# A planned attention, Fourier and feed-forward kernel on one core: shared work is left to ScalarE or GpSimd where they end it in time, and two batches are transposed earlier

## The chip, the cores and the metric

The kernel runs on one core of a Trainium2 chip. The core has a matrix engine (PE, with weight loads on PEld), a vector engine (DVE), a scalar engine (ACT), GpSimd (POOL) and a queue engine (SP); they run beside each other and wait for each other by semaphores. The metric is the time of one execution in microseconds (us) on the device, less is better; three runs of the kernel before are given by their median.

## The reference

Four batches of 576 tokens, 8 heads of 64, width 512. Attention with random features comes first: `phi(x) = exp(proj - max)`, `kv = k_p^T v`, output `(q_p kv) / (q_p z)`. Two layers follow:

```python
X = np.fft.fft(np.fft.fft(x, axis=1), axis=2)          # layer one
u = x + np.real(X)
un = (u - mean) / sqrt(var + 1e-6)
x = u + relu(un @ w_ch1) @ w_ch2                        # 512 -> 2048 -> 512

h = x.transpose(0, 2, 1) @ U @ V                        # layer two, U 576x32, V 32x576
u = x + h.transpose(0, 2, 1)
out = u + relu(u @ w_ch1) @ w_ch2
```

Weights come as 64-bit floats and are converted on the chip. Every matmul is done in pairs of a high and a low part (`xh`, `xl`), so one product costs three matmuls: high by high, high by low, low by high.

## The kernel before, in words

**Stages.** Attention runs over 36 tiles of 128 tokens (`proj`, `exps`, then `kvmm` for keys, `qtr`, `num` and `xtr` for queries). For query tile n, `pt` transposes phi, a copy to `qpT` on ACT or DVE follows, `pn` multiplies it with kv, DVE divides (`den`, `x`), and `px` transposes the result, which a copy puts into `uT`, the residual (512 x 2304, transposed). The Fourier stage runs as filling work in between: `fold` (z tiles), `ps` and `pdp`/`pdq` matmuls, and DVE or POOL adds into `uT`. The feed-forward part works on six blocks of 384 tokens: 0, 1, 3 and 4 are the first 384 tokens of the four batches, blocks 2 and 5 the last 192 of batches 0 and 1 and of batches 2 and 3. Its first hidden columns run unit by unit (`phu`, `acc`, functions `l1`, `l2`), and all others in cells (`loop`): a cell (J, p) is weight group J on the pair p of blocks, (0, 1), (2, 5) or (3, 4); it has four hidden products of 12 matmuls (`ph`) and seven output products of 6 (`p`), which DVE adds into `uT`. Cells 0 to 17 are layer one, 18 to 35 layer two.

**Between the layers** stands `rec_mix(b)` for each batch b (the two thin products with U and V): for five token tiles PE transposes `uT` (`mt`), ACT writes a high part, DVE the low part, PE adds them up with U (`pg`); then ACT and DVE make `g2`, and eight matmuls with V (`pu`) follow, each added into `uT` by DVE. `pu` has two PSUM banks, so the third waits until DVE has added the first. Then `rec_x2` makes the input tiles `yh` (ACT) and `yl` (DVE or POOL) of a block.

**What sets the order.** No engine schedules itself. Every step is recorded with `add`: a set of engines that may do it with a cost each, and keys that it reads and writes. `Sched.plan` gives each step a latest start (`lst`), counted back from the PE work in its recorded place, then walks through time and lets the engine that is free first take, among the steps that are ready, the one with the smallest `lst`. A step with several engines (a copy on A or V, a subtraction on V or G) goes to whichever takes it. Steps with `lock` on VectorE and GpSimd are kept apart in time. What comes out is a fixed program for each engine. So a changed rule or key moves thousands of instructions.

Of the kernel before, what the change touches and what calls it, by code (L numbers as in the profile page):

```python
# [91 lines left out]
ENGS = "XPAVGSD"  # L92

# [5 lines left out]
class Sched:  # L99
# [8 lines left out]
    def add(self, eng, fn, r=(), w=(), lock=False, main=False, early=0.0, slack=0.0):  # L108
# [5 lines left out]
        o.preds, o.succs, o.raw, o.slack = set(), [], set(), slack  # L114
# [14 lines left out]
        self.ops.append(o)  # L129

    def plan(self):
        ops = self.ops
        for i, o in enumerate(ops):
            for p in o.preds:
                ops[p].succs.append(i)
            o.left, o.on, o.lst, o.after = len(o.preds), None, None, None
# [6 lines left out]
        for o in reversed(ops):  # L143
# [4 lines left out]
            o.lst = (min(v) if v else t) - o.early  # L148
        chain = [i for i, o in enumerate(ops) if o.main]
# [34 lines left out]
        while len(order) < n:  # L184
# [84 lines left out]
def tile_favor_fnet_moe(ctx: ExitStack, tc: tile.TileContext, qT, kT, v1, om, w1a, w2a, uu, vv, w1b, w2b, cs, cd, out):  # L269
# [90 lines left out]
    plb = ca.enter_context(tc.tile_pool(name="plb", bufs=1))  # L360
# [10 lines left out]
    CE = (("ce",), CA)  # L371
    C1 = CE[0]
# [38 lines left out]
    def load(n):  # L411
# [4 lines left out]
        def fn(e):  # L416
# [4 lines left out]
            if n:  # L421
                nc.sync.dma_start(r, src)
# [7 lines left out]
        add({"S": S256 if n else 1.7}, fn, [C1], [("rw", n % 3)] + ([] if n else [("sa",)]))  # L430

    def load_v(n):
# [16 lines left out]
        add({"S": S256}, fn, [C1], [("vt", i % 3)])  # L449

    def om_prep():
        def sc(e):
            nc.scalar.activation(M["omr"], M["omr"], AF.Copy, scale=SCALE)
# [5 lines left out]
        add({"A": 0.32}, sc, [], [("sa",)])  # L459
# [17 lines left out]
    def proj(n, g):  # L477
# [24 lines left out]
        add({"V": V512}, red, [("pj", b), CP, CA], [("mx", n % 2, g)])  # L502

    def exps(n, g):
        if n >= NS:
            return
        for h0 in (4 * g, 4 * g + 2):
# [11 lines left out]
    def kvmm(n, i):  # L519
# [24 lines left out]
    def qtr(n, g):
# [14 lines left out]
        add({"A": 0.49, "V": V512}, cpy, [("pm", q), CE[n % 2], CA], [("qpT", n % 2, g)])  # L559

    def num(n, g):
# [33 lines left out]
        add({"V": 0.08}, div, [bank, CA] + bx, [("den", g)])  # L595
# [29 lines left out]
    def fold(n, src, rk, key):  # L625
# [49 lines left out]
    def s_stage(b, kd, kind):  # L675
# [1107 lines left out]
```

## Time and profile before

| | before |
|---|---|
| median of 3 runs | 1034.96 us (1033.78 to 1038.09) |
| the profiled execution, its span | 1032.16 us, 1030.4 us |
| PE, PEld busy | 98 %, 95 % |
| DVE, ACT, POOL busy | 86 %, 51 %, 37 % |
| matmuls | 6240 |

The span runs from the first to the last instruction; 1.76 us of the execution lie around it. The busy time of PE counts a matmul until its modelled end, so matmuls that follow each other closely overlap (a 128x384 one is shown with 0.34 us but starts 0.17 us after the one before), and an idle stretch of PE is a little shorter in the table than what the wait costs.

### The profile page before, as it was taken

The numbers are of one execution on the slowest core, as the hardware profiler recorded it, in microseconds if no ns is written. First come the engines' busy times: TensorE is split into PE (matmuls) and PEld (weight loads), VectorE is DVE, ScalarE is ACT, GpSimd is POOL, SyncE is SP. The second block draws the span as 40 slices with busy tenths as digits, with TensorE's granted clock in tenths as the row PEclk, the third lists the DMA queues.
The fourth block names the chain that finished last, engine by engine and source line by source line (L and its number), as shares of the span: only waits on it lengthen the run. The fifth ranks groups of instructions, "written<-read, shape, count | busy, mean of one in ns | idle before, by whom it ended". The sixth has DMA issues, their size and how long they took to land.

```text
span 1030.4 us, 17155 instructions
## 1 busy us (share of the span) xinstructions
PE 1007.1 (98%) x6240; PEld 983.6 (95%) x6240; DVE 883.7 (86%) x1906; ACT 522.6 (51%) x1212; POOL 380.2 (37%) x396
## 2 busy tenths in 40 slices
PE   9999999898999999999999999999999999999998
PEld 8999998898999999999999998889999999999997
DVE  5788999677888999989899888998999898987766
ACT  6797888634444443444442565544554354443232
POOL 2266235412414334424332371524543343433211
PEclk9999999999999999999999998999999999999999
DMA  6445230010112110011110201002121111010013
GB/s 190 139 165 164 74 93 11 9 34 21 42 41 86 58 48 10 30 49 35 62 41 21 62 21 42 21 22 83 42 62 41 42 41 63 26 37 1 1 62 122
DMA packets 49091, 57.01 MB, mean 55 GB/s; under 512 B 3120, under 2 KB 42160, under 8 KB 48880
## 3 DMA queue, kind: packets, MB, share of 16 engines
q1 hardware_dynamic: 48720, 53.23, 16.9%
q0 software_dynamic: 288, 2.70, 0.7%
q8 instruction: 49, 0.80, 0.3%
q14 instruction: 34, 0.28, 0.1%
HBM read 51.20 MB, written 4.72 MB: 54 GB/s over the span
## 4 chain that ended last, share of the span: by engine, by line
PE 88%; DVE 7%; ACT 2%; POOL 1%; issue 1%; DMA 0%; SPq 0%; DVEq 0%; ACTq 0%; POOLq 0%
PE ph L1007 11%; PE ph L1008 11%; PE ph L1006 11%; PE p L1267 10%; PE p L1265 10%; PE p L1266 10%; PE pj L397 4%; PE kvp L397 3%; DVE uT L382 2%; PE acc L1043 1%; PE acc L1042 1%; PE acc L1044 1%; PE phu L1006 1%; PE phu L1007 1%; PE phu L1008 1%; PE pn L397 1%
## 5 line engine op out<-in xcount | busy, mean ns | idle before, releaser
L382 DVE TENSOR_TENSOR uT<-uT,p 128x384 f32<-128x384 f32 x588 | 308.3, 550 | 57.0 <-PE p L1267 56.0
L312 POOL TENSOR_TENSOR w<-w,sc 128x512 uint32<-128x512 uint32 x64 | 87.7, 1372 | 149.0 <-DVE w L308 118.3
L1006 PE MATMUL ph<-yh,ah 128*128 128x384 f32 x384 | 130.3, 339 | 0.6 <-ACT yh L388 0.6
L1007 PE MATMUL ph<-yl,ah 128*128 128x384 f32 x384 | 129.9, 338 | 0.7 <-DVE yl L382 0.7
L1008 PE MATMUL ph<-yh,al 128*128 128x384 f32 x384 | 129.9, 338 | 0.0
L1267 PE MATMUL p<-hl,bh_s 128*128 128x384 f32 x294 | 99.6, 339 | 0.2 <-DVE hl L382 0.2
L1265 PE MATMUL p<-hh,bh_s 128*128 128x384 f32 x294 | 99.0, 337 | 0.0
L1266 PE MATMUL p<-hh,bl_s 128*128 128x384 f32 x294 | 98.8, 336 | 0.0
L1006 PE MATMUL ph<-xh,ah 128*128 128x384 f32 x288 | 97.1, 337 | 0.0
L1008 PE MATMUL ph<-xh,al 128*128 128x384 f32 x288 | 96.8, 336 | 0.0
L1007 PE MATMUL ph<-xl,ah 128*128 128x384 f32 x288 | 96.8, 336 | 0.0
L512 ACT ACTIVATE phi<-pj,mx 128x128 f32<-128x128 f32 x288 | 82.5, 386 | 16.6 <-DVE mx L499 16.4
L388 ACT ACTIVATE r<-ph 128x384 f32<-128x384 f32 x66 | 32.5, 492 | 103.1 <-PE ph L1008 103.0
L388 ACT ACTIVATE hh<-t 128x384 fp32r<-128x384 f32 x72 | 37.9, 526 | 82.1 <-DVE t L991 78.9
L382 POOL TENSOR_TENSOR hl<-r,hh 128x384 fp32r<-128x384 f32 x36 | 39.9, 1107 | 100.6 <-ACT hh L388 92.3
L1006 PEld LDWEIGHTS ph<-yh,ah 128*128 128x128 f32 x384 | 72.7, 189 | 1.7 <-ACT yh L388 0.8
L1007 PEld LDWEIGHTS ph<-yl,ah 128*128 128x128 f32 x384 | 72.6, 189 | 1.1 <-DVE yl L382 1.0
L1008 PEld LDWEIGHTS ph<-yh,al 128*128 128x128 f32 x384 | 72.6, 189 | 0.0
L388 ACT ACTIVATE hh<-f 128x384 fp32r<-128x384 f32 x60 | 31.6, 526 | 79.5 <-PE p L1266 25.1
L1265 PE MATMUL p<-hh,bh_a 128*128 128x384 f32 x210 | 71.0, 338 | 0.1
L1266 PE MATMUL p<-hh,bl_a 128*128 128x384 f32 x210 | 70.7, 336 | 0.0
L1267 PE MATMUL p<-hl,bh_a 128*128 128x384 f32 x210 | 70.6, 336 | 0.0
(724 smaller groups left out, 2873.1 us busy)
## 6 DMA issues: line engine op xcount, KB each, us to landing
raw<-in_w1a_dram SPq DMA_DIRECT2D x16, 512.0 KB, 3.7
raw<-in_w2a_dram SPq DMA_DIRECT2D x16, 512.0 KB, 3.7
raw<-in_w2b_dram SPq DMA_DIRECT2D x16, 512.0 KB, 3.5
raw<-in_w1b_dram SPq DMA_DIRECT2D x16, 512.0 KB, 3.7
raw<-in_qT_dram SPq DMA_DIRECT2D x18, 256.0 KB, 3.0
out_dram<-uT SPq DMA_DIRECT2D x24, 192.0 KB, 2.0
raw<-in_kT_dram SPq DMA_DIRECT2D x17, 256.0 KB, 3.0
vt<-in_v_dram SPq DMA_DIRECT2D x16, 260.0 KB, 2.7
```

The lines of the kernel that those rows point to most:

```text
L312: sch.ins = aeng.tensor_tensor(out=mu, in0=mu, in1=s, op=ALU.add).ins
L382: sch.ins = ENG[e].tensor_tensor(out=o, in0=x, in1=y, op=op).ins
L388: nc.scalar.activation(o, x, fn)
L397: nc.tensor.matmul(o, w, m, start=start, stop=stop, skip_group_check=True)
L512: nc.scalar.activation(phi_[n][:, h, :], pj_[(n, g)][:, h - 4 * g, :], AF.Exp, bias=mx_[n][:, h : h + 1])
L1006: nc.tensor.matmul(ph, wh[:, c], xh[:, r, :], start=(r == 0), stop=False)
L1007: nc.tensor.matmul(ph, wh[:, c], xl[:, r, :], start=False, stop=False)
L1008: nc.tensor.matmul(ph, wl[:, c], xh[:, r, :], start=False, stop=(r == 3))
L1042: nc.tensor.matmul(a, wh[:, c], hh, start=(f == 0), stop=False)
L1265: nc.tensor.matmul(a, wh[:, cc], hh, start=first, stop=False, skip_group_check=True)
L1266: nc.tensor.matmul(a, wl[:, cc], hh, start=False, stop=False, skip_group_check=True)
L1267: nc.tensor.matmul(a, wh[:, cc], hl, start=False, stop=True, skip_group_check=True)
```

## The change

**The rule.** In `plan`, VectorE has chosen a step that another engine may also do. If some other engine x would end that step before its latest start (plus what PE is late; ScalarE gets 1.0 us more), VectorE takes the most urgent ready step that only VectorE can do instead. If there is none it keeps the step. `MIX` holds one entry that does nothing.

**The start.** The small matrix `om` is loaded on ScalarE's queue; the loads of input tile 2 and of the first values are recorded behind its scaling.

**Attention.** `xtr` (`px`) is recorded ahead of the second half of `num` (`pn`). Some keys are made finer or added.

**Block 2.** Its layer-one input tiles get an own pool (`xpc`), opened in the place of attention tiles when these are done, where they had to wait for the end of the whole Fourier stage (`close_a`); so `lnu_c(2)` and `lnu_v(2)` are recorded earlier. The tiles `mm` and `pmm` move to another pool.

**Between the layers.** The last two weight groups of layer one are interleaved, so blocks 0 and 1 are done with four cells to go (three before). Batches 0 and 1 get own tiles for the transposes (in the layer-one input tiles of blocks 0 and 1), and their first three token tiles are recorded from there; on PE the three transposes of batch 1 now stand in cell 16 instead of 17, some 115 to 145 matmul instructions earlier. Batches 2 and 3 begin with their last two token tiles.

```diff
+GS = 0.0
+GA = 0.0
+AS = 1.0
...
+            if e == "V" and l > GA and any(max(free[x], avail(i, x)) + o.eng[x] < l + late + (GS if x == "G" else AS) for x in o.eng if x != e):
+                alt = [x for x in now if len(ops[x[1]].eng) == 1]
+                if alt:
+                    l, i, v = min(alt)
+                    o = ops[i]
...
-                if p == 0:
-                    M["omr"] = lnp.tile([128, 512], F32, tag="sa", name="omr")[:, 0:256]
-                    nc.sync.dma_start(M["omr"], om)
...
+    def load_om():
+        def fn(e):
+            M["omr"] = lnp.tile([128, 512], F32, tag="sa", name="omr")[:, 0:256]
+            nc.scalar.dma_start(M["omr"], om)
...
-    cells += [(J, p) for pp in ((0, 1), (2,)) for J in (NP - 2, NP - 1) for p in pp]
+    cells += [(J, p) for p in range(3) for J in (NP - 2, NP - 1)]
...
-        pool = xps[0 if blk < 2 else 1]
+        pool = M["x2"] if blk == 2 else xps[0 if blk < 2 else 1]
...
+    def close_c(e):
+        c2.close()
+        M["x2"] = ctx.enter_context(tc.tile_pool(name="xpc", bufs=1, side="right", reuse_waits="tile"))
...
     def rec_mix(b):
+        own = b < 2
+        order = TILES if own else TILES[3:] + TILES[:3]
...
+            add({"P": 0.3}, tr, [("u", r, b, "h" if t < 3 else "t") for r in range(4)] + [mk], [("m", 1)])
+            add({"A": A512}, nh, [("m", 1), mk], [("nh", k)])
+            add({"V": 0.62}, nl, [("m", 1), ("nh", k), mk], [("nl", k)])
...
+            if own and s == 2:
+                yield
...
+            if (J, p) == (NP - 1, 0):
+                mx = [rec_mix(b) for b in range(4)]
+                for b in (0, 1):
+                    next(mx[b])
             if (J, p) == (NP - 2, 2):
                 for b in (0, 1):
-                    rec_mix(b)
+                    next(mx[b], None)
...
+                if s > 10:
+                    xtr(n - 2)
                 if s > 9:
                     num(n - 1, 1)
                 qtr(n, 1)
                 exps(m, 1)
-                if s > 10:
-                    xtr(n - 2)
...
                 lnu_rs(1)
                 lnu_mean(2)
+                lnu_c(2, True, True)
+                lnu_v(2)
...
-        lnu_c(2, True, True)
-        lnu_v(2)
```

PE has the same 5870 matmul instructions before and after. DVE has 1908 instructions before and 1828 after, ACT 1214 and 1219, POOL 401 and 477. Three places show what moved; in the order the names are those of the program, with the numbers of tile, batch or cell.

PE in the attention stage, query tiles 33 to 35, before (`pt34_0` transposes, `pn33_1` is the second half of the product of tile 33, `pj35_1` the projection of tile 35):

```order
L397 MATMUL pn33_0_2695<-kv3_2118,qpT33_2655 128x65 x4
L609 MATMUL px31_2707<-ident_58,x31_2557 128x128 x3
L609 MATMUL px31_2707<-ident_58,xr31_2609 128x128
L550 MATMUL pt34_0_2718<-ident_58,phi34_2644 128x128 x4
L397 MATMUL pn33_1_2725<-kv3_2118,qpT33_2655 128x65 x4
L397 MATMUL pj35_1_2736<-omh_119,th35_2554 128x256
L397 MATMUL pj35_1_2736<-oml_120,th35_2554 128x256
```

and after:

```order
L570 MATMUL pt34_0_2714<-ident_58,phi34_2644 128x128 x4
L413 MATMUL pj35_1_2727<-omh_115,th35_2525 128x256
L413 MATMUL pj35_1_2727<-oml_116,th35_2525 128x256
L413 MATMUL pj35_1_2727<-omh_115,tl35_2526 128x256
L413 MATMUL pj35_1_2727<-omh_115,th35_2525 128x256
L413 MATMUL pj35_1_2727<-oml_116,th35_2525 128x256
L413 MATMUL pj35_1_2727<-omh_115,tl35_2526 128x256
L629 MATMUL px32_2743<-ident_58,x32_2641 128x128 x3
L629 MATMUL px32_2743<-ident_58,xr32_2725 128x128
L413 MATMUL pn33_1_2750<-kv3_2123,qpT33_2658 128x65 x4
```

The second half `pn33_1` came straight behind `pt34_0`; now the six matmuls of `pj35_1` and the transposes `px32` stand between them.

DVE where the low parts of block 2's input (`xl2`) are made, before (`hht7_0` belongs to unit 7, the last before block 2's first unit 8):

```order
L382 TENSOR_TENSOR hht7_0_3634<-acc4_0_3291,rs1_3196 128x384
L382 TENSOR_TENSOR xl2_3632<-c2_0True_3403,xh2_3631 128x384
L382 TENSOR_TENSOR xl2_3632<-c2_1True_3409,xh2_3631 128x384
L382 TENSOR_TENSOR c2_2True_3643<-uT_67,mean2_3206 128x384
L382 TENSOR_TENSOR c2_3True_3648<-uT_67,mean2_3206 128x384
L382 TENSOR_TENSOR s2_3_3652<-uT_67 128x384
L382 TENSOR_TENSOR q2_0_3411<-q2_0_3411,q2_2_3650 128x384
L382 TENSOR_TENSOR xl2_3632<-c2_2True_3643,xh2_3631 128x384
L382 TENSOR_TENSOR q2_0_3411<-q2_0_3411,q2_3_3656 128x384
L382 TENSOR_TENSOR xl2_3632<-c2_3True_3648,xh2_3631 128x384
```

and after (`hlu3`, `hlu4` are the low hidden parts of units 3 and 4):

```order
L1018 SCALAR_TENSOR_TENSOR hlu3_3192<-phu3_3145,hhu3_3177 128x384
L398 TENSOR_TENSOR xl2_3190<-c2_0True_3179,xh2_3189 128x384
L398 TENSOR_TENSOR c2_2True_3207<-uT_67,mean2_3166 128x384
L398 TENSOR_TENSOR xl2_3190<-c2_1True_3184,xh2_3189 128x384
L398 TENSOR_TENSOR q2_0_3194<-q2_0_3194,q2_1_3205 128x384
L398 TENSOR_TENSOR c2_3True_3222<-uT_67,mean2_3166 128x384
L398 TENSOR_TENSOR q2_0_3194<-q2_0_3194,q2_2_3214 128x384
L398 TENSOR_TENSOR abl_2_3_3132<-ps2_3o_3168,abh_2_3_3131 128x2x144
L398 TENSOR_TENSOR q2_0_3194<-q2_0_3194,q2_3_3236 128x384
L398 TENSOR_TENSOR xl2_3190<-c2_2True_3207,xh2_3189 128x384
L398 TENSOR_TENSOR xl2_3190<-c2_3True_3222,xh2_3189 128x384
```

`xl2` stood behind unit 7; now all four are done before the hidden part of unit 4.

DVE at the end of layer one, from the last adds of cell 17 (`p17`) to the adds of batch 1's `pu1`, before (`w36` and `w39` are weights under conversion):

```order
L382 TENSOR_TENSOR uT_67<-uT_67,p17_0_1_7713 128x384
L915 TENSOR_SCALAR w36_7448<-w36_7448 128x512
L382 TENSOR_TENSOR uT_67<-uT_67,pu1_0_7878 128x288
L382 TENSOR_TENSOR uT_67<-uT_67,pu1_1_7880 128x288
L308 SCALAR_TENSOR_TENSOR w36_7448<-raw36_7394,w36_7448 128x512
L382 TENSOR_TENSOR uT_67<-uT_67,pu1_2_7889 128x288
L382 TENSOR_TENSOR uT_67<-uT_67,pu1_3_7892 128x288
L382 TENSOR_TENSOR uT_67<-uT_67,pu1_4_7899 128x288
L382 TENSOR_TENSOR uT_67<-uT_67,pu1_5_7902 128x288
L911 TENSOR_SCALAR w39_7718<-w39_7718 128x512
L382 TENSOR_TENSOR uT_67<-uT_67,pu1_6_7905 128x288
L382 TENSOR_TENSOR uT_67<-uT_67,pu1_7_7911 128x288
```

and after:

```order
L398 TENSOR_TENSOR uT_67<-uT_67,p17_5_1_7886 128x384
L398 TENSOR_TENSOR uT_67<-uT_67,p17_0_0_7743 128x384
L398 TENSOR_TENSOR uT_67<-uT_67,pu1_1_7917 128x288
L398 TENSOR_TENSOR uT_67<-uT_67,pu1_0_7920 128x288
L398 TENSOR_TENSOR uT_67<-uT_67,p17_0_1_7755 128x384
L398 TENSOR_TENSOR uT_67<-uT_67,pu1_3_7943 128x288
L398 TENSOR_TENSOR uT_67<-uT_67,pu1_2_7945 128x288
L398 TENSOR_TENSOR uT_67<-uT_67,pu1_5_7954 128x288
L398 TENSOR_TENSOR uT_67<-uT_67,pu1_4_7958 128x288
L398 TENSOR_TENSOR uT_67<-uT_67,pu1_7_7963 128x288
L398 TENSOR_TENSOR uT_67<-uT_67,pu1_6_7966 128x288
```

The three conversion steps between the `pu1` adds are gone, and one add of `p17` stands between the first pair and the rest. On PE all eight `pu1` matmuls followed each other behind the 12 of `ph18_0`; now two stand behind the first three of these 12, and six behind all of them.

## Rows read from the trace of the kernel before

**Rows 1.** The page: an engine's busy time, and the chain that ended last.

```profile
PE 1007.1 (98%) x6240; PEld 983.6 (95%) x6240; DVE 883.7 (86%) x1906; ACT 522.6 (51%) x1212; POOL 380.2 (37%) x396
...
PE 88%; DVE 7%; ACT 2%; POOL 1%; issue 1%; DMA 0%; SPq 0%; DVEq 0%; ACTq 0%; POOLq 0%
```

**Rows 2.** Windows: start:end, length, busy of PE, PEld, DVE, ACT, POOL (instructions), clock, DMA.

```profile
0.00:100.00 100.00, 95.32 (x787) 92.25 (x788) 72.20 (x167) 76.40 (x232) 43.51 (x56) 1.00 0.54 166
150.00:200.00 50.00, 44.46 (x357) 41.09 (x357) 39.18 (x107) 39.45 (x108) 22.14 (x24) 1.00 0.04 11
200.00:250.00 50.00, 48.32 (x306) 47.04 (x305) 37.21 (x86) 19.31 (x42) 12.04 (x19) 1.00 0.11 33
250.00:300.00 50.00, 47.63 (x276) 45.35 (x275) 45.14 (x96) 23.09 (x50) 14.07 (x13) 1.00 0.14 43
300.00:600.00 300.00, 300.00 (x1725) 297.26 (x1724) 272.45 (x577) 131.57 (x272) 115.13 (x111) 1.00 0.14 43
600.00:650.00 50.00, 47.84 (x256) 42.50 (x255) 44.65 (x92) 31.61 (x65) 18.70 (x19) 0.93 0.14 43
650.00:700.00 50.00, 47.44 (x267) 43.85 (x266) 46.06 (x98) 23.55 (x49) 20.14 (x20) 1.00 0.05 13
700.00:1000.00 300.00, 300.00 (x1719) 299.79 (x1719) 258.27 (x533) 131.19 (x268) 111.70 (x109) 1.00 0.13 42
```

**Rows 3.** Timeline of the start: start, length, engine, line, operation, count, idle before and releaser.

```profile
7.63 0.42 DVE L382 TENSOR_TENSOR oml<-omr,omh 128x256 fp32r<-128x256 f32 x1
...
7.96 0.68 DVE L499 TENSOR_REDUCE mx<-pj 128x4 f32<-128x512 f32 x1
...
9.88 0.38 PE L397 MATMUL pj<-omh,th 128*128 128x256 f32 x1 [0.92 <-ACT phi L512]
```

**Rows 4.** Waits of PE, 60 to 240 us: total, times, longest.

```profile
PE px L609 <- DVE abl L382: 1.8, 2, 1.4
PE pt L550 <- ACT phi L512: 1.4, 3, 0.8
```

**Rows 5.** Timeline of PE at block 2's first hidden product.

```profile
252.04 0.45 PE L1006 MATMUL phu<-xh,ah 128*128 128x384 f32 x1
...
257.66 0.34 PE L1006 MATMUL phu<-xh,ah 128*128 128x384 f32 x1
```

**Rows 6.** Timeline of PE at two `pu` stretches and behind the second.

```profile
603.14 0.43 PE L1496 MATMUL pu<-vh,mxl 96*128 96x288 f32 x2
603.41 0.34 PE L1006 MATMUL ph<-xh,ah 128*128 128x384 f32 x1
```

**Rows 7.** Timeline of PE at batch 1's `pu` and the first `yh` of block 1.

```profile
625.81 0.43 PE L1496 MATMUL pu<-vh,mxl 96*128 96x288 f32 x2
...
630.76 1.11 PE L1454 MATMUL mt<-ident,uT 128*128 128x128 f32 x4 [0.55 <-DVE uT L382]
631.52 0.67 PE L1006 MATMUL ph<-yh,ah 128*128 128x384 f32 x1
...
635.51 0.68 PE L1454 MATMUL mt<-ident,uT 128*128 128x128 f32 x4
```

**Rows 8.** Timeline of DVE beside it.

```profile
627.14 0.69 DVE L308 SCALAR_TENSOR_TENSOR w<-raw,w 128x512 uint32<-128x512 uint32 x1
627.74 1.80 DVE L382 TENSOR_TENSOR uT<-uT,pu 128x288 f32<-128x288 f32 x4
629.47 0.42 DVE L911 TENSOR_SCALAR w<-w 128x512 f32<-128x512 f32 x1
```

**Rows 9.** Window behind it, columns as in rows 2.

```profile
631.50:635.50 4.00, 4.00 (x14) 3.91 (x13) 3.73 (x8) 2.16 (x4) 0.00 (x0) 0.50 0.00 0
```

**Rows 10.** Groups by line and form: count, busy us, mean ns, idle before.

```profile
L382 DVE TENSOR_TENSOR uT<-uT,p 128x384 f32<-128x384 f32 x588 | 308.3, 550 | 57.0 <-PE p L1267 56.0
...
L382 DVE TENSOR_TENSOR hl<-r,hh 128x384 fp32r<-128x384 f32 x60 | 35.6, 593 | 5.6 <-ACT hh L388 5.5
```

**Rows 11.** The same view, of POOL.

```profile
L382 POOL TENSOR_TENSOR hl<-r,hh 128x384 fp32r<-128x384 f32 x36 | 39.9, 1107 | 100.6 <-ACT hh L388 92.3 <-issue 6.5 <-DVE hl L382 1.1
```

More of the change, by code (lines that the diff above doesn't have):

```diff
@@ L106, in __init__, with add @@
         self.ins = None
-    def add(self, eng, fn, r=(), w=(), lock=False, main=False, early=0.0, slack=0.0):
+    def add(self, eng, fn, r=(), w=(), lock=False, main=False, early=0.0, slack=0.0, after=None):
         if not self.on:
@@ L133, in plan @@
         for i, o in enumerate(ops):
+            if o.after is not None:
+                o.preds.add(o.after)
             for p in o.preds:
                 ops[p].succs.append(i)
[L136 removed]
+            o.left, o.on, o.lst = len(o.preds), None, None
         t = 0.0
@@ L148, in plan @@
             o.lst = (min(v) if v else t) - o.early
+        for i, o in enumerate(ops):
+            k = max(j for j in range(len(MIX)) if MIX[j][0] <= o.lst)
+            if MIX[k][1] and not o.main:
+                o.lst += MIX[k][2] * (((i + 1) * 2654435761 + MIX[k][1] * 2246822519) % 65521 / 65521 - 0.5)
         chain = [i for i, o in enumerate(ops) if o.main]
@@ L409, in warm, with load @@
             add({"P": 0.45 * WARM}, fn, [CA], [("pm", 0)])
-    def load(n):
+    def load(n, after=None):
         if n >= NS:
@@ L691, in fn @@
             for c in range(2):
-                zh, zl = zs_[f"{b}{kind}{c}"]
+                zh, zl = (zs_[f"{b}{kind}{c}"][i] for i in range(2))
                 ch = cs_[:, 0, c, i0 : i0 + 2 * w]
@@ L711, in s_stage @@
         add({"P": 1.08}, fn, zk + [("cst",), CA], [("pm", q)])
-        add({"A": 0.3}, hi, [("pm", q), CA], [("abh", sl, kind)])
+        add({"A": 0.3}, hi, [("pm", q), CA], [("abh", sl, kind)] + ([(x, sl, y) for x in ("abh", "abl") for y in "eo"] if kind == "e" else []))
         add({"V": 0.38}, lo, [("pm", q), ("abh", sl, kind), CA], [("abl", sl, kind)])
@@ L1437, in rec_mixc, with tiles, bufs, g2t @@
             add({"V": 0.4}, lambda e, vs=vs: tt("V", b["vh"][64:96, vs], b["vr"][64:96], b["vh"][64:96, vs].bitcast(F32), ALU.subtract), [("sq", 1)], [("vh",)], lock=True)
+    MX = {}
     def rec_mix(b):
         x = {}
[L1442 to L1452 removed]
+        own = b < 2
+        mk = ("mx", b) if own else ("mx", 2)
+        order = TILES if own else TILES[3:] + TILES[:3]
+        def tiles():
+            k = b if own else 2
+            if k not in MX:
+                blk = b if own else 5
+                MX[k] = [xps[0 if own else 1].tile([128, 3, 512], F32R, tag=f"x{i}{blk}", name=f"mx{i}{k}") for i in "hl"]
+            return MX[k]
+        def bufs(s):
+            ta, tb = tiles()
+            if own:
+                return ta[:, s % 3], tb[:, s % 3]
+            return ((ta[:, 0], ta[:, 1]), (ta[:, 2], tb[:, 0]))[s % 2]
+        def g2t():
+            ta, tb = tiles()
+            return ta[0:96, 2] if own else tb[0:96, 1 + b % 2]
+        if b != 3:
+            add({"X": 0.0}, lambda e: tiles(), [], [mk] + [("x", b if own else 5, r) for r in range(4)])
+        nb = 3 if own else 2
+        for s, (t0, n) in enumerate(order):
+            t = t0 // 128
+            if own and s == 3:
+                for q in range(3):
+                    x[q]()
+                x["q"] = 3
+            def tr(e, s=s, t0=t0, n=n):
+                x["pt"] = bank(f"mt{b}_{s}", ("m", 1)).rearrange("p (r d) -> p r d", r=4)
@@ L1477, in gs1 @@
+            x[s] = lambda s=s, k=k, pgm=pgm: add({"P": 0.46}, pgm, [("nh", k), ("nl", k), ("ust",), mk], [("m", 0)])
+            if not (own and s < 3):
+                for q in range(x.get("q", 0), s + 1):
+                    x[q]()
+                x["q"] = s + 1
+            if own and s == 2:
+                yield
         def gs1(e):
@@ L1658, in whole @@
         num(NS - 1, 0)
+        xtr(NS - 2)
         num(NS - 1, 1)
-        xtr(NS - 2)
         for p in fill.get(NS - 1, []):
             p()
+        add({"X": 0.0}, close_c, [], [C2] + [("x", 2, r) for r in range(4)])
         lnu_rs(0)
```

125 lines of the change are left out of this document (60 added, 65 removed).

## The prediction

> **What bounds the kernel now.** I read the page first. PE is busy 98 % of the span, and the chain that ended last runs through PE for 88 % [rows 1]. PE's instructions are the same after the change, so time can be won only where PE waits or runs slowly. The windows show where that is [rows 2]. From 300 to 600 and from 700 to 1000 us PE is busy all the time: nothing to win there, only to lose. It idles 4.7 us in the first 100 us, 5.5 from 150 to 200, 1.7 from 200 to 250, 2.4 from 250 to 300, and 2.2 and 2.6 in the two windows from 600 to 700, where the layers meet. A wait costs more than its idle time, because the overlap of pipelined matmuls is lost: a 128x384 matmul is shown with 0.34 us [rows 5] but follows the one before after 300/1725 = 0.174 us [rows 2], so I add 0.17 us for each wait that goes.
>
> In the stretches with idle time I looked at PE's waits and at the timelines of PE and DVE. The reader is to see there that PE is always held by something short: a copy, a maximum, a subtraction on DVE or ACT that stands too late in its engine's order. DVE is busy 272 of 300 us and 258 of 300 us in the quiet stretches and POOL 115 and 112 [rows 2], so DVE is the engine that is short of room and POOL has some.
>
> **The change part by part.** All terms are sums against the profiled execution of 1032.16 us, which is 2.8 us below the median of 1034.96; I add the 2.8 at the end.
>
> The start. PE waits 0.92 us at 9.88 for an exponential, which waits for the first maximum on DVE at 7.96, and this stands directly behind `oml` at 7.63 (0.33 us from start to start) [rows 3]. In the new order `oml` is DVE's first step, while DVE still waits for input, so the maximum moves up by that 0.33 us; the `om` load no longer stands among SP's first loads, so tile 1's comes up by one issue as well. Against it: ACT issues a DMA before its table load, ACT now also makes tile 2's high part between its first exponentials, and the loads of tile 2 and of the first values wait for ACT's scaling. Bounds: 0.9 lost to 1.3 won. I take 0.8 won.
>
> Attention, 60 to 240 us. PE waits there in many short pieces, the largest two groups being 1.8 us in two waits of `px` and 1.4 us in three waits of `pt` [rows 4]. The order puts the projection (six matmuls) and `px` between `pt` and the second `pn`, so the copy between them has that much longer, and DVE's work becomes more even: in the order, 27 instructions stood between the maxima of tiles 16 and 17 and 28 between those of 34 and 35; now it is 13 and 14. But the waits for the z tiles (`ps` on `zl`) keep about the same distance, and shifting shared steps leaves some of them to POOL, where a subtraction takes 1.11 us on average against 0.59 on DVE [rows 10, 11]. The idle time to be had is 2.2 us before 100 (4.7 less 1.5 for the first instruction and the 0.9 above), 5.5 and 1.7 later, together 9.4 us. Bounds: everything goes (9.4 won, and 0.17 for each of some 17 waits, 12 in all), or new waits of the same size arise elsewhere (0, or 3 lost by a third more). In between no row decides; I take a bit less than half of the 12: 5.3 won.
>
> Block 2. From 252.04 to 257.66 us PE does 12 matmuls and takes 5.62 us [rows 5]; at 0.174 each they take 2.1. The rest, 3.5 us, is waiting for `xl2` and `xh2`, whose tiles came free only with the Fourier stage. In the new order all four `xl2` steps stand before the hidden part of unit 4, while block 2 starts with unit 8: four units of 24 matmuls, some 17 us, lie between. What is late next is `prs2`, needed only when block 2's results are scaled. I take 3.5 won; bounds 2.5 to 3.5.
>
> Between the layers. The eight `pu` of batch 1 and the four transposes behind them take from 625.81 to 631.52, 5.71 us [rows 7]. Their own work is 8 times 0.135 (two took 0.27 in an undisturbed place [rows 6]) and 0.38 for the transposes (half of 0.76, at half clock), together 1.46; 4.25 us are lost, because each pair waits for DVE's two adds, and between these stand steps of weight conversion, which nobody needs soon: 0.60 us for one, from 627.14 to 627.74 [rows 8]. In the new order these are gone, two of the eight are done under cover of `yh0` matmuls, and six remain in a row. Four adds took 1.73 us (627.74 to 629.47) [rows 8], so three pairs take 2.6, with the transposes 3.0 us; their own work is 1.2, so 1.8 us are lost and 2.4 won. While PE stood in these gaps its clock fell: from 631.5 to 635.5 it was granted 0.50, the lower of its two levels, 1.2 GHz [rows 9]. 12 matmuls took 3.99 us there (631.52 to 635.51 [rows 7]) instead of 2.1: 1.9 us. With three pairs in place of four and nine full matmuls behind the first pair I expect PE to stay at 2.4 GHz, so these 1.9 are won too. Should the clock fall all the same, nothing of the 1.9 is won.
>
> For batches 2 and 3 (640 to 681 us) the order keeps `pu` in rows (eight in a row became rows of up to six for batch 3, where it had been three); DVE has as many adds as before. Batch 1's transposes moved out of cell 17 into cell 16, so DVE comes out of cell 17 with 45 instructions where it had 54. I take 0.6 won here. Bounds for the border of the layers as a whole: 1 lost (longer rows at batch 3, the clock falls anyway) to 8 won (all of the 4.7 us idle [rows 2] with nine waits, and the 1.9 of the clock). I take 2.4 + 1.9 + 0.6 = 4.9.
>
> The cells. Some 62 of POOL's 76 additional instructions stand in the cells, mostly low parts of weights, which are made a group ahead, and about 13 `hl` and `yl`, which PE needs soon. The rule hands a step over only if POOL ends it before its latest start on DVE. In the trace PE never waited in the cells although POOL made 36 `hl<-r` there at 1.11 us [rows 2, 11]. I take 0.5 lost for two or three late ones; bounds 0 to the rival below.
>
> Beside POOL, DVE's own `hl<-r` takes 593 ns in the mean where its add of a PSUM result takes 550 [rows 10]; 76 more POOL steps that slow one DVE step each by this 43 ns cost DVE 3 us in all, off PE's path. Against this change stands a rule: the Trainium skill (SBUF — State Buffer, Who interferes with whom) says that a VectorE instruction with two SBUF inputs and a GpSimd instruction that reads SBUF contend, and that the second waits until the first has ended. The trace bears it out in kind, with 43 ns in the mean. Taken at its word it is the last rival's mechanism, whose price is worked out there from rows.
>
> The sum: 0.8 + 5.3 + 3.5 + 4.9 - 0.5 = 14.0. 1032.2 - 14.0 + 2.8 = 1021.0 us.
>
> **The rivals.**
> *All waits go.* Then 0.9 at the start, 12 in attention, 3.5 and 8 are won: 24.4, that is 1010.6 us. For it speaks that DVE's peaks are halved; against it that six `pu` in a row and the chain from maximum to exponential to transpose are still there.
> *The waits of attention only move.* The static order was already the planner's best guess before; its costs differ from the trace, so new waits arise where old ones went. Then block 2's 3.5 and 2.4 at the border are won, 1.5 are lost elsewhere: 4.4, that is 1030.6 us. For it speaks that every wait there is well under 2 us, the size of the planner's error.
> *Late results from POOL (slower).* Place: the cells, where PE has no idle time to hide it. Each of the 62 added steps there ends 1.107 - 0.593 = 0.51 us later than on DVE [rows 10, 11]. If each held PE by that, 32 us would be lost and 14.5 won elsewhere: 1035 - 14.5 + 32 = 1052 us. It decides from 14.5/62 = 0.23 us per step. Against it speaks that weights are made early; for it that a DVE step which comes while POOL works may have to wait as well.
>
> **How the numbers follow.** Forecast 0.60, with its own range 1015 to 1027; all waits go 0.16; the waits move 0.17; slower 0.07. Of the forecast's range nearly all is over 0.5 % (5.2 us, about what a measurement here can tell from no change) below 1035, the second rival straddles that line (two fifths below it). Faster 0.59 + 0.16 + 0.05 = 0.80, slower 0.06, the same 0.14. The range that holds eight in ten takes in the first two rivals: 1009 to 1031.
>
> **What would show it.** PE idle per window: near 0 from 250 to 300; under 3 us from 150 to 200; no stretch of 0.50 clock near 630, and about 3 us from the third `pu` of batch 1 to the first `yh` of block 1. In the cells no PE wait for `hl`, `yl` or weights of over 0.3 us. The prediction would be wrong if PE's busy time stayed at its idle sums of before in attention, or if waits on POOL appear between 300 and 600 us.

## The result and the profile after

The changed kernel takes 1021.65 us (median of four runs, 1020.36 to 1025.25), the kernel before 1036.41 us beside it; the ratio is 0.9875 with an interval of 0.9848 to 0.9903. The forecast was 1021.0 us. The profiled execution is the longest of the four, 1025.25 us with a span of 1023.5, so between the two profiles only 6.9 us are gone. The total came out; not all of its parts did.

The page of the changed kernel, busy time and chain, as in [rows 1]:

```profile
PE 1007.7 (98%) x6240; PEld 989.8 (97%) x6240; DVE 853.7 (83%) x1826; ACT 526.2 (51%) x1216; POOL 442.5 (43%) x472
...
PE 90%; DVE 5%; ACT 2%; POOL 1%; issue 1%; DMA 0%; SPq 0%; DVEq 0%; ACTq 0%; POOLq 0%
```

DVE has 80 instructions fewer and POOL 76 more; PE does the same as before (6240 matmuls in both traces), and DVE's share of the chain falls from 7 to 5 %. The windows, with the columns of [rows 2]:

```profile
0.00:100.00 100.00, 97.94 (x826) 96.45 (x827) 79.29 (x180) 80.10 (x243) 45.76 (x60) 1.00 0.57 169
150.00:200.00 50.00, 47.92 (x346) 46.38 (x347) 32.50 (x89) 35.75 (x97) 25.77 (x29) 0.86 0.02 6
200.00:250.00 50.00, 46.71 (x290) 45.48 (x289) 38.86 (x89) 21.21 (x47) 16.98 (x27) 0.97 0.09 27
250.00:300.00 50.00, 50.00 (x299) 49.20 (x297) 40.49 (x90) 23.46 (x47) 16.16 (x15) 1.00 0.16 49
300.00:600.00 300.00, 300.00 (x1732) 298.13 (x1732) 268.73 (x557) 133.77 (x277) 141.63 (x142) 1.00 0.16 48
600.00:650.00 50.00, 49.00 (x276) 43.70 (x276) 43.24 (x90) 31.92 (x66) 29.32 (x33) 1.00 0.04 11
650.00:700.00 50.00, 48.28 (x263) 45.30 (x262) 44.47 (x90) 25.31 (x50) 18.77 (x17) 0.97 0.15 43
700.00:1000.00 300.00, 300.00 (x1721) 299.81 (x1720) 245.94 (x507) 127.56 (x261) 126.55 (x129) 1.00 0.12 38
```

Against [rows 2] PE idles less wherever it did idle, but for one stretch: from 200 to 250 us it is 3.3 us where it was 1.7. And from 150 to 200 the mean clock is 0.86 where it was 1.00, so PE is busy for longer and does less (346 matmuls, 357 before). PE's longest waits from 60 to 240 us, columns as in [rows 4]:

```profile
PE ps_0e L718 <- ACT zh3e L404: 2.8, 1, 2.8
PE pt L570 <- ACT phi L532: 0.9, 1, 0.9
PE prs L909 <- ACT uT L404: 0.7, 1, 0.7
```

The waits of [rows 4] have shrunk (`pt`, 1.4) or gone (`px` on `abl`, 1.8); a new one of 2.8 us, for the last Fourier fold (`zh3e`), is the longest of all. Three windows of the changed kernel show the clock:

```profile
150.00:164.00 14.00, 14.00 (x67) 14.00 (x68) 6.14 (x18) 7.72 (x22) 8.87 (x10) 0.51 0.07 19
631.50:635.50 4.00, 4.00 (x24) 3.71 (x24) 3.54 (x7) 3.57 (x8) 1.85 (x3) 1.00 0.29 98
670.00:677.00 7.00, 5.71 (x21) 4.86 (x22) 6.08 (x11) 3.91 (x9) 3.55 (x4) 0.76 0.00 0
```

The 0.50 at 631.5 [rows 9] is gone: 24 matmuls in those 4 us, where 14 were. Instead 1.2 GHz was granted for 13.65 us from 150.10 on, and for 3.41 us from 232.02 and from 672.34 on.

The border of the layers, PE, timeline as in [rows 7]:

```profile
623.13 0.43 PE L1554 MATMUL pu<-vh,mxh 96*128 96x288 f32 x2
623.98 0.76 PE L1554 MATMUL pu<-vh,mxh 96*128 96x288 f32 x2 [0.41 <-DVE uT L398]
624.92 0.76 PE L1554 MATMUL pu<-vh,mxh 96*128 96x288 f32 x2 [0.18 <-DVE uT L398]
625.87 0.66 PE L1504 MATMUL mt<-ident,uT 128*128 128x128 f32 x4 [0.18 <-DVE uT L398]
626.30 0.44 PE L1033 MATMUL ph<-yh,ah 128*128 128x384 f32 x1
```

and DVE beside it, as in [rows 8]:

```profile
623.47 2.71 DVE L398 TENSOR_TENSOR uT<-uT,pu 128x288 f32<-128x288 f32 x6
```

Six adds in a row with no weight step between them; from the third `pu` to the first `yh` 3.17 us.

Where the time goes in each kernel is seen best from the starts of the same matmuls. The table counts matmuls by name in each trace (`kvp 10` is the tenth `kvp`); it gives the start less that in the kernel before, in us, and for each profiled execution its mean granted clock. `kvp 10` stands behind the start, `pj 350` and `pj 400` in attention, `phu 73` near the end of the Fourier stage (block 2 begins with `phu 97`). The cells of layer one lie between `phu 200` and `ph 800`, the border of the layers between `ph 800` and `ph 1000`, the cells of layer two behind it. The experiments e1 to e12 follow below.

| kernel | median | clock | kvp 10 | pj 350 | pj 400 | phu 73 | phu 200 | ph 800 | ph 1000 | span |
|---|---|---|---|---|---|---|---|---|---|---|
| before (start) | 1036.4 | 0.996 | 11.64 | 143.04 | 166.82 | 226.86 | 293.39 | 587.75 | 688.59 | 1030.4 |
| changed | 1021.7 | 0.990 | -1.5 | -4.2 | +0.9 | -1.0 | -2.5 | -2.7 | -6.7 | -6.9 |
| e9, changed again | 1020.8 | 0.992 | -1.4 | -4.2 | -2.3 | -4.2 | -5.5 | -5.8 | -9.4 | -9.6 |
| e1, no rule | 1029.9 | 0.993 | -1.5 | -4.3 | -5.9 | -4.8 | -6.8 | -1.5 | -0.8 | -0.7 |
| e2, old border | 1024.2 | 0.987 | -1.5 | -4.2 | +0.9 | -1.0 | -2.3 | -3.0 | -3.2 | -3.4 |
| e3, old block 2 | 1027.9 | 0.990 | -1.4 | -4.2 | -3.8 | -6.4 | -1.0 | -1.2 | -3.2 | -3.4 |
| e4, old px | 1040.1 | 0.987 | -1.3 | +3.1 | +7.5 | +12.1 | +11.8 | +11.6 | +8.5 | +8.1 |
| e5, no rule, old border | 1026.1 | 0.988 | -1.4 | -4.3 | -5.8 | -3.3 | -5.4 | -4.4 | -2.8 | -2.3 |
| e6, no rule, old px | 1038.4 | 0.993 | -1.4 | -0.2 | -0.5 | +3.6 | +0.1 | +5.3 | +5.8 | +5.6 |
| e7, block 2 later | 1020.5 | 0.994 | -1.6 | -4.3 | -5.5 | -7.9 | -9.1 | -9.4 | -11.6 | -11.8 |
| e8, rule from 200 us | 1018.8 | 0.995 | -1.4 | -4.2 | -5.8 | -7.1 | -9.2 | -9.5 | -13.2 | -13.4 |
| e10, fold free | 1016.4 | 0.996 | -1.5 | -4.4 | -5.9 | -6.7 | -13.5 | -13.3 | -17.5 | -17.6 |
| e11, fold free, rule all | 1016.8 | 0.997 | -1.2 | -3.9 | -3.5 | -5.0 | -11.8 | -11.6 | -16.5 | -16.7 |
| e12, old start | 1024.8 | 0.992 | -0.5 | -3.1 | -1.2 | -3.3 | -3.3 | -2.8 | -6.2 | -6.3 |

### The profile page after: what moved, and what is told of

The parts are those of the page before. It is cut to its first block, busy times and chain, and to the rows that moved or that the text cites. A ratio compares the mean times of both kernels' runs of the same rounds, so it can differ in the third digit from the quotient of the medians.

```text
span 1023.5 us, 17183 instructions
## 1 busy us (share of the span) xinstructions
PE 1007.7 (98%) x6240; PEld 989.8 (97%) x6240; DVE 853.7 (83%) x1826; ACT 526.2 (51%) x1216; POOL 442.5 (43%) x472
## 4 chain that ended last, share of the span: by engine, by line
PE 90%; DVE 5%; ACT 2%; POOL 1%; issue 1%; DMA 0%; SPq 0%; DVEq 0%; ACTq 0%; POOLq 0%
PE ph L1034 11%; PE ph L1033 11%; PE ph L1035 11%; PE p L1292 10%; PE p L1294 10%; PE p L1293 10%; PE pj L413 4%; PE kvp L413 3%; PE pn L413 2%; PE acc L1069 2%; PE acc L1070 1%; PE acc L1071 1%; PE phu L1033 1%; PE phu L1035 1%; PE phu L1034 1%; DVE uT L398 1%
## 5 line engine op out<-in xcount | busy, mean ns | idle before, releaser
L328 POOL TENSOR_TENSOR w<-w,sc 128x512 uint32<-128x512 uint32 x64 | 83.6, 1310 | 136.1 <-DVE w L324 51.8
L398 POOL TENSOR_TENSOR hl<-r,hh 128x384 fp32r<-128x384 f32 x44 | 49.5, 1124 | 96.0 <-ACT hh L404 73.0
L532 ACT ACTIVATE phi<-pj,mx 128x128 f32<-128x128 f32 x288 | 83.6, 389 | 12.2 <-DVE mx L519 11.6
```

Source lines behind the costliest of these rows:

```text
L328: sch.ins = aeng.tensor_tensor(out=mu, in0=mu, in1=s, op=ALU.add).ins
L398: sch.ins = ENG[e].tensor_tensor(out=o, in0=x, in1=y, op=op).ins
L532: nc.scalar.activation(phi_[n][:, h, :], pj_[(n, g)][:, h - 4 * g, :], AF.Exp, bias=mx_[n][:, h : h + 1])
```

## The experiments

**e1, the rule alone off.**

```diff
-GA = 0.0
+GA = 1e9
```

> The changed kernel, its planner rule alone switched off (GA = 1e9); all other edits stay. Theory A, the rule makes the gain in attention (5.3 us of the forecast) and costs 0.5 in the cells: about 4.8 us longer than the changed kernel's 1021.7, 1026.5 us, ratio to before about 0.992, with PE waiting 3 to 5 us more between 60 and 240 us. Rival B, the new order of px and projection makes that gain and the rule moves work that nobody waits for: within 1.5 us of 1021.7, ratio 0.986 to 0.989. Rival C, the rule's late results on POOL cost more in the cells than it wins: 1017 to 1020, ratio under 0.985.

1029.91 us (1028.57 to 1031.72), ratio 0.9939 [0.9916, 0.9962]. The rule is worth 8 us, but not where theory A put it: up to pj 350 the two kernels agree within 0.1 us. With the rule off PE loses 5.3 us between phu 200 and ph 800, in the cells, and from there to ph 1000, at the border, 0.7 where the changed kernel wins 4.0. Its waits in the cells, 500 to 550 us (total, times, longest):

```profile
PE p L1294 <- DVE hl L398: 1.6, 3, 0.7
PE p L1292 <- DVE uT L398: 0.7, 1, 0.7
PE p L1292 <- ACT hh L404: 0.6, 2, 0.4
```

None of these exists in the changed kernel. All three theories were wrong on the place.

**e2, the border as before**: `rec_mix` in one piece in the two shared tiles, and

```diff
-    cells += [(J, p) for p in range(3) for J in (NP - 2, NP - 1)]
+    cells += [(J, p) for pp in ((0, 1), (2,)) for J in (NP - 2, NP - 1) for p in pp]
```

> The changed kernel with the border of the layers as in the kernel before: batches 0 and 1 mix in one piece in the two shared tiles behind cell 17, the cells of the last group in their old order. Theory A (term of 4.9 us): the eight pu in a row and the half clock near 630 us come back, 4.5 to 5 us longer than the changed kernel, 1026 to 1027 us, ratio 0.991 to 0.992. Rival B, the rule alone empties DVE there so that the pairs of adds come in time: within 1.5 us of 1021.7, ratio 0.986 to 0.989, and the stretch of eight pu takes about 3 us instead of 5.7.

1024.24 us (1021.17 to 1028.83), ratio 0.9871 [0.9833, 0.9910], an interval that holds the changed kernel's ratio too: by the medians 2.6 us longer, where theory A had 4.5 to 5. The trace is clearer: from ph 800 to ph 1000 this kernel wins 0.2 us against before, the changed one 4.0. From ph 865 to ph 877 (the first `yh` of block 0 and of block 1, with the `pu` of batch 1 between) it takes 7.29 us (7.79 before, 5.51 changed). 3.41 us at 1.2 GHz are back too, from 628.45 on. Rival B is out, theory A stands with half its size.

**e3, block 2's input late again**: `lnu_c(2)` and `lnu_v(2)` behind `close_a`, the tiles in the pool that opens there.

```diff
-        pool = M["x2"] if blk == 2 else xps[0 if blk < 2 else 1]
+        pool = xps[0 if blk < 2 else 1]
```

> The changed kernel with block 2's input made late again, in the pool that opens behind the Fourier stage. Theory A (term of 3.5 us): the 12 matmuls after the start of block 2 take 5.6 us again, 3 to 3.5 us longer than the changed kernel, 1025 us, ratio about 0.990. Rival B, the early steps of block 2 on DVE and POOL are what delays the fold at 228 to 235 us (a wait of 2.8 us and a stretch at half clock): undone, that wait goes and 1.7 at half clock with it, so the sum is within 1.5 us of 1021.7, ratio 0.986 to 0.989.

1027.94 us (1027.04 to 1028.88), ratio 0.9917 [0.9886, 0.9949]: 6.3 us longer, twice theory A's 3 to 3.5. The 12 matmuls from phu 97 to phu 109 take 9.58 us, not 5.6. PE's waits from 240 to 262 us:

```profile
PE phu L1033 <- POOL xl L398: 1.8, 1, 1.8
PE phu L1032 <- ACT xh L404: 1.6, 2, 0.8
PE phu L1033 <- DVE xl L398: 0.5, 1, 0.5
```

and 10.24 us at 1.2 GHz from 249.16 on. Rival B was right in its mechanism and wrong in its sum: the wait for `zh3e` falls from 2.8 to 0.3 us without the early steps, but block 2 then costs more.

**e4, px in its old places**, behind the exponentials; `xtr(NS - 3)` and `xtr(NS - 2)` likewise.

```diff
                 proj(m, 1)
-                if s > 10:
-                    xtr(n - 2)
...
                 exps(m, 1)
+                if s > 10:
+                    xtr(n - 2)
```

> The changed kernel with px (the transposes of attention's result) in its old places, behind the exponentials and behind the first projections; the rule stays. Theory A, rule and order of px share attention's 5.3 us, the order about half: 2 to 3 us longer than the changed kernel, 1024 us, ratio 0.989 to 0.9905, with the waits of px on abl (1.8 us in two before) back. Rival B, the order is the whole gain: 5 us longer, ratio 0.992. Rival C, the order moves nothing: within 1 us of 1021.7.

1040.09 us (1037.60 to 1041.71), ratio 1.0032 [1.0009, 1.0055]: 18 us longer than the changed kernel, and no faster than the kernel before (at a clock of 0.988 its runs take 1038.9 to 1039.4 us, before 1038.8 to 1039.3). No theory had this. PE's largest wait from 60 to 240 us was 1.0 us in the kernel before:

```profile
PE pn L413 <- DVE x L605: 7.8, 3, 4.7
```

The longest of the three, on DVE (start, length):

```profile
182.41 0.43 DVE L398 TENSOR_TENSOR e22o<-eo_1o 128x256 f32<-128x256 f32 x1 [0.77 <-POOL z2o L398]
...
186.97 0.42 DVE L398 TENSOR_TENSOR z2e<-eo_1e 128x256 f32<-128x256 f32 x1
187.31 0.15 DVE L600 TENSOR_SCALAR den<-pn 128x4 f32<-128x4 f32 x1
...
189.06 0.72 DVE L605 TENSOR_TENSOR x<-pn,den 128x256 f32<-128x256 f32 x2
```

PE had ended the last `pn` at 183.4 and the work behind it at 184.95; it stands 4.66 us until 189.60, when `x` lets the next `pn` go. DVE first does a row of fold steps, from 182.41 to 187.3, and before it waits 0.77 us for a fold step on POOL. These are shared steps. In e6 below, without the rule, the waits for `x` are two, 2.0 us together, the longest 1.5; but there `pn` waits 4.3 us for `phi`, so a part of the wait has moved.

**e5, rule off and the old border.** The edits of e1 and e2 together.

> Rule off and the border of the layers as before; the start, the place of px and block 2's early input stay new. Theory A: the new order of the last group's cells asks for one cell's weights a cell earlier and adds the early transposes, so DVE runs short of room near 500 us, and the rule is what pays for it. Then without both, the waits for hl and uT from 518 to 532 us (5 us with the rule off) are gone, PE loses under 1 us from 500 to 600 us, and the eight pu in a row return: 1024 to 1027 us, 3 to 6 us shorter than with the rule off alone (1029.9). Rival B: the waits at 518 to 532 come from weights that the missing rule leaves on DVE whatever the order; they stay, and the time is 1030 to 1034 us.

1026.14 us (1022.75 to 1029.91), ratio 0.9920 [0.9891, 0.9949]. Theory A: 516 to 534 us in e1,

```profile
516.00:534.00 18.00, 15.09 (x77) 12.80 (x76) 17.95 (x39) 10.11 (x21) 6.93 (x8) 1.00 0.22 68
```

in e5,

```profile
516.00:534.00 18.00, 18.00 (x105) 18.00 (x104) 17.81 (x38) 7.19 (x14) 6.76 (x6) 1.00 0.19 61
```

and in the changed kernel:

```profile
516.00:534.00 18.00, 18.00 (x105) 18.00 (x104) 17.15 (x36) 7.07 (x15) 10.20 (x12) 1.00 0.08 30
```

In e1 DVE is busy 17.95 of 18 us and PE idles 2.9. The old order of the cells takes the demand away, the rule takes work away: POOL's 6.93 us become 10.20. The new cells cost some 4 us up to ph 800 (e1 loses 5.3 from phu 200 on, e5 1.0), and the rule pays them back. (A wait for `hl` of 0.5 us at 539 stays in e5.)

**e6, rule off and px old.** The edits of e1 and e4 together.

> Rule off and px in its old places. Theory A: the rule does harm only where px stands in its old places (rule on, px old: 1040 us), because it then leaves PE's next input behind other steps; without the rule the old places cost what they cost before, so PE's pj 350 stands within 1.5 us of the kernel before's 143.0 (138.8 with both edits, 146.1 with the rule alone), and the whole takes 1032 to 1036 us. Rival B: the old places of px are the harm by themselves, with the other new edits around them: pj 350 at 145 to 147 us again and 1038 us or more.

1038.37 us (1035.04 to 1040.80), ratio 1.0038 [1.0017, 1.0059]. A's mechanism held (pj 350 at 142.89 us, 143.0 expected), its total did not: I forgot that with the rule off the cells lose their 5 us, as in e1 (phu 200 to ph 800: 5.2).

**e7, block 2 later.**

```diff
                 lnu_mean(2)
-                lnu_c(2, True, True)
-                lnu_v(2)
+            if s == 4:
+                lnu_c(2, True, True)
+            if s == 6:
+                lnu_v(2)
```

> The changed kernel, block 2's c, q and xl steps asked for two pieces later and its variance sum four, so that the last Fourier fold comes first on DVE. Theory A: the wait of 2.8 us for zh3e at 228 us goes, the half clock behind it (3.4 us) too, and block 2 still starts without a wait: 4 to 5 us shorter than the changed kernel, 1017 us, ratio 0.982 to 0.984. Rival B: the fold is late for another reason (POOL idles there for 10 us and does not help), the wait stays at 2 us or more, and the time is within 1 us of 1021.7. Rival C: block 2's xl2 comes late on POOL, PE waits 1 to 2 us at the start of unit 8: 1019 to 1022 us with the wait at 228 gone.

1020.52 us (1019.98 to 1022.50), ratio 0.9869 [0.9844, 0.9894]. The wait for `zh3e` is still 1.9 us. Theory A fell: block 2's steps are not the only reason.

**e8, the rule from 200 us on.**

```diff
-GA = 0.0
+GA = 200.0
```

> The changed kernel with its rule working only from 200 us of the planner's time on (the first instruction it moves is at about 220 us). Theory A: the rule's gain lies in the cells (5 us at 518 to 532) and at the border (3 us), nothing of it in attention: 1018 to 1022 us, ratio 0.983 to 0.988, no wait in the cells. Rival B: the rule is needed in attention as well, since without it the waits for zh2e and zl2e at 172 us and the half clock behind them cost 5 us: 1024 to 1027 us, ratio 0.988 to 0.992.

1018.79 us (1018.28 to 1021.30), ratio 0.9857 [0.9831, 0.9884]. Theory A: without the rule in attention nothing is lost, and the cells stay free of waits (-0.3 us from phu 200 to ph 800, as in the changed kernel). Whether it is better than the changed kernel, the runs don't tell.

**e9, the changed kernel again.** No edit.

> The changed kernel once more, without an edit. Theory A: the stretch of 13.65 us at half clock from 150 us on belongs to that one execution and not to the kernel (the same instructions showed 13.65, 3.41 and no half clock there in the profiles of three kernels that share them), so pj 400 now stands near 161.4 us instead of 167.7 if the stretch is absent, and the time of each run follows its mean granted clock: 1020 to 1021 us at 0.995 to 0.996, 1022.5 at 0.993, 1025 at 0.990. Rival B: the kernel's waits at 148 and 149 us bring the stretch every time: pj 400 at 166 to 168 us again and all runs between 1020 and 1026 us without relation to the clock.

1020.84 us (1019.45 to 1022.53), ratio 0.9855 [0.9830, 0.9881]. Neither theory was right: the stretch at half clock came again, half as long. The window from 150 to 164 us in e9,

```profile
150.00:164.00 14.00, 14.00 (x103) 13.79 (x104) 8.49 (x24) 10.24 (x30) 8.82 (x10) 0.76 0.07 19
```

and in e7, which has the same instructions up to there:

```profile
150.00:164.00 14.00, 14.00 (x137) 13.56 (x138) 11.41 (x32) 13.11 (x40) 10.79 (x13) 1.00 0.07 20
```

67, 103 and 137 matmuls in the same 14 us. The part of A on the runs held: with the mean granted clock at 0.996 they take 1019.45 and 1020.36 us, at 0.993 1021.35 and 1022.49, at 0.990 1025.25.

**e10, the fold free**: the edits of e7 and e8, and the fold's pieces in one group.

```diff
-        (21, "aDr1 bF0evvv"),
-        (22, "bF0ovvv bF1evvg bF1ovgv"),
+        (21, "aDr1 bF0evvv bF1evvg bF0ovvv bF1ovgv"),
```

> The changed kernel with the rule from 200 us of the planner's time on, the last fold's pieces ahead of the first hidden result, with which they share two buffers, and block 2's input and sums two and four pieces later. Theory A: the fold was late because its second half waits for those buffers, not for room on DVE or POOL; the wait for zh3e (2.06 us with the rule from 200 on), the one for zl3e (0.5) and the half clock behind them (3.4 us) go: 3.5 to 4.5 us shorter than the 1018.8 of the rule from 200 on, 1014.5 to 1015.5 us, ratio about 0.981. Rival B: DVE is full there whatever the buffers; the wait moves to the hidden part or to zl3o, 1017.5 to 1019 us.

1016.43 us (1014.57 to 1018.45), ratio 0.9819 [0.9791, 0.9847]; all five runs are below the five of e9 beside them. DVE in the changed kernel:

```profile
223.59 0.54 DVE L398 TENSOR_TENSOR t<-acc,rs 128x384 f32<-128x384 f32 x1
224.06 0.67 DVE L398 TENSOR_TENSOR eo_0o<-x,x 128x512 f32<-128x512 f32 x1
```

and in e10:

```profile
208.71 0.69 DVE L397 TENSOR_TENSOR eo_0o<-x,x 128x512 f32<-128x512 f32 x1
...
214.69 1.02 DVE L397 TENSOR_TENSOR t<-acc,rs 128x384 f32<-128x384 f32 x2
```

`eo` and `t` take turns in the same two tiles. Recorded behind `t`, the odd half of the fold had to wait for the first hidden result; recorded ahead, it is done 15 us sooner (5.8 of them because all of PE's work is earlier), and PE's waits from 200 to 262 us are down to one:

```profile
PE pdq3r L755 <- DVE pmm3r L397: 0.2, 1, 0.2
```

The span is 4.2 us shorter than e8's, the median 2.4, where theory A had 3.5 to 4.5: its mechanism stands, its size nearly. This kernel also makes block 2's steps later; the fold alone is the difference between e7 and e11.

**e11, the same with the rule from the beginning**: e10 with `GA = 0.0`.

> The same early fold and later block 2, with the rule working from the beginning as in the changed kernel. Theory A: the fold's wait goes here too (1.88 us for zh3e in the version with block 2 later), and the rule gives nothing in attention: 1016 to 1018 us, 0 to 2 us above the same with the rule from 200 us on. Rival B: the rule is worth something there, 1 us or more below that version.

1016.78 us (1015.44 to 1017.94), ratio 0.9813 [0.9788, 0.9838]: theory A, the same as e10. It differs from e7 only in the order of the fold's pieces, and is 3.7 us shorter by the medians. The waits for `zh3e` and `zl3e` (1.9 and 0.6 us in e7) are gone, and from phu 73 to phu 200 it wins 6.7 us where e7 wins 1.2.

**e12, the start as before**: `om` among SP's first loads again, nothing held back for ACT.

> The changed kernel with the start as before: om among SP's first loads, no load held back for ACT's scaling. Theory A (term of 0.8 us): kvp 10 stands 0.8 to 1.5 us later than the changed kernel's 10.16 us, and all later marks with it up to 140 us: 1 us longer in all. Rival B: the place of oml alone makes the gain (it is DVE's first step in both), kvp 10 within 0.3 us of 10.16.

1024.78 us (1022.44 to 1025.86), ratio 0.9890 [0.9860, 0.9920]. Theory A at kvp 10, which stands 1.0 us later (11.17 us). The whole is longer by more than the 1 us expected; up to phu 73 it stays 0.9 to 1.1 us behind e9, and behind that the two traces differ by a longer stretch at half clock (6.83 us from 229.49, 3.41 in e9) and by 0.8 us in the cells, where the planned order is another too. So the rest of the difference can't be put down to the loads of the start.

## Why the prediction was right or wrong

**The total came out, in part by luck.** The sum stood on the profiled execution of the kernel before, which had a mean clock of 0.996, and went from there to the median by adding 2.8 us; it had no term for the clock of the runs. Runs at an equal clock compare better: at 0.993 the kernel before took 1034.0 to 1034.8 us in five runs, the changed one 1021.35 and 1022.49; at 0.995 1033.2 and 1033.4 against 1020.82. The change is worth some 12.5 us at the same clock; the sum said 14.0. The medians lie 14.8 us apart; part of the rest is that the changed kernel's runs had the higher clock (0.9937 in the mean of nine, 0.9924 in the mean of 48 of the kernel before), and whether the change itself raises it is not shown. The terms were off in both directions and nearly cancel: 1.5, 5.8 to 6.4, 1.5, 4.0 and +0.3 us were measured (attention in kernels without half clock there) for 0.8, 5.3, 3.5, 4.9 and -0.5. In the chances, two fifths of the second rival's 0.17 are 0.07, where 0.05 was added.

All the signs that the prediction named for its steps were there (PE idle 0 from 250 to 300 us and 2.1 from 150 to 200, no half clock near 630): they told where time goes, not by which edit.

**The start**, 0.8 forecast: 1.5 won at kvp 10, 1.0 of it by the new loads (e12).

**Attention**, 5.3 forecast. Without the stretch at half clock the size is right: from kvp 10 to phu 73 e7 wins 6.4 and e8 5.8 us. In the profiled run the 13.65 us at 1.2 GHz gave it all back (0.5 lost). The step that failed is the cause: beside px's new place it counted on DVE's more even work, which I took for the rule's doing (theory A of e1). e1 and e6 differ only in px, by 4.2 us at pj 350 and 8.4 at phu 73, with 6.83 us at half clock in both: more than the whole term. The changed kernel and e1 differ only in the rule, by 0.1 at pj 350. With px in its old place the rule even costs 3.2 us there and 8.5 by phu 73 (e4 against e6), of which about 5 is, as an estimate, half of the 10.24 us that e4 has more at half clock up to there.

**Block 2**, 3.5 forecast, bounds 2.5 to 3.5. At the place itself it came: 12 matmuls from phu 97 to phu 109 take 2.76 us, 5.62 before [rows 5]. But from phu 73 to phu 97 PE loses 2.7 us, the wait for the fold. Up to phu 200 1.5 us are left. The step "what is late next is `prs2`" was wrong: next was the fold, whose DVE steps the early `xl2` steps were put ahead of (e3), and whose second half stood behind two shared tiles (e10, e11). That I read no row on it cost 2 us of the forecast; with the fold freed e10 and e11 win 6.7 us from phu 73 to phu 200.

**The border**, 2.4 + 1.9 + 0.6 = 4.9 forecast: 4.0 measured from ph 800 to ph 1000. The drain of `pu`: 2.3 won from ph 865 to ph 877 (2.4 forecast), with 3.17 us from the third `pu` (3 forecast). The clock: 1.3 from ph 877 to ph 889 in place of 1.9. Batches 2 and 3: 2.1 won up to ph 961, then 2.0 lost in the new stretch at half clock at 672, 0.2 for 0.6. What I missed is that it takes both parts: from ph 800 to ph 1000 the new border without the rule loses 0.7 us (e1), the rule without the new border wins 0.2 (e2), and with neither 1.6 are lost (e5). The whole runs at a clock of 0.993 say the same: 1021.35 and 1022.49 us with both, 1023.4 and 1023.7 with the rule alone, 1025.6 and 1026.1 with neither, 1030.3 to 1031.7 with the new border alone. So the rule is worth some 9 us with the new border and 2.3 with the old one.

**The cells**, 0.5 lost forecast: 0.3 won, and no wait for `hl`, `yl` or weights from 300 to 600 us. The term was nearly right and its reading wrong. I took the 62 steps on POOL for a small cost without a use, since PE never waited there before. They are what the new order of the cells needs (e1, e5). The rival of late results from POOL is out: POOL's `hl<-r` still takes twice DVE's time [rows 10, 11], but is handed over only where there is time. The groups after, on DVE and on POOL:

```profile
L398 DVE TENSOR_TENSOR uT<-uT,p 128x384 f32<-128x384 f32 x588 | 308.0, 548 | 75.1 <-PE p L1294 74.8
...
L398 DVE TENSOR_TENSOR hl<-r,hh 128x384 fp32r<-128x384 f32 x52 | 29.6, 570 | 5.1 <-ACT hh L404 4.9
...
L398 POOL TENSOR_TENSOR hl<-r,hh 128x384 fp32r<-128x384 f32 x44 | 49.5, 1124 | 96.0 <-ACT hh L404 73.0
```

With 76 more steps on POOL DVE's `hl<-r` takes 570 ns in the mean, not more than the 593 of [rows 10]. The prediction's 43 ns on each step was a wrong reading of that mean: the median of `hl<-r` is 556 ns before and after, and a few instructions take up to 1085 ns (before) and 1210 ns (after). The longest one after, and the POOL instruction beside it:

```profile
756.53 1.31 POOL L328 TENSOR_TENSOR w<-w,sc 128x512 uint32<-128x512 uint32 x1 [3.15 <-DVE r L398]
757.04 1.21 DVE L398 TENSOR_TENSOR hl<-r,hh 128x384 fp32r<-128x384 f32 x1
```

The DVE step ends 0.41 us behind the end of POOL's. The same holds for every one of DVE's `hl` and `yl` steps from two SBUF tiles that takes over 600 ns (nine before, seven after): each starts while a POOL instruction runs and ends 0.41 to 0.42 us behind that one's end. The Trainium skill (SBUF — State Buffer, Who interferes with whom) lets such an instruction with two SBUF inputs contend with a GpSimd instruction that reads SBUF; these traces agree. What the rival feared exists, but it met few steps, and PE waited for none of them from 300 to 600 or from 700 to 1000 us.

**The rivals.** "The waits of attention only move" is half true: one moved wait, the fold, took 2.8 us and some of the clock. "All waits go" is where e10 and e11 point; they still wait at the border.

## What to carry to other kernels

A rule that takes work off a busy engine paid most here (9 us against 2.3) where another part of the change asks more of that engine; undo each part alone and in pairs before crediting one. When a step is made earlier, ask which buffers its neighbours share and what it is put ahead of. Where the granted clock differs between executions, compare runs of equal clock, and two profiles by the starts of the same instructions.

## What was not expected of the hardware

The same instructions, with the same waits of 0.88 and 0.22 us at 148 to 150 us, were followed by 13.65 (changed, e2), 6.83 (e9), 3.41 (e3, e11) and no (e7) us at 1.2 GHz. Where the rule is off in attention these waits are 0.23 to 0.25 us each, and no stretch followed at that place in four executions (e1, e5, e8, e10). But these four have waits of 0.9 to 1.0 and 0.7 us between 173 and 175.3 us instead, and there stretches of 6.83 (e1, from 175.9) and 10.24 us (e5, from 175.0) at 1.2 GHz began, none in e8 and e10. So the table's profiled executions differ by such stretches as well as by the edits. What decides their length between executions of one program stays open. Over all runs of the kernel before, a mean clock of 0.997 goes with 1031 to 1032 us and 0.984 with 1044.
